# One-token attention with an MLP beside it, on one core: V taken in pairs, block sums masked on VectorE, activations stationary in the query and first MLP products

## The chip, the cores and the metric

The kernel runs on one core of a Trainium2 chip. The metric is the device time of one execution in microseconds (us). Three executions of the kernel before gave a median of 368.69 us (368.61 to 369.18). A profiled execution gives the trace; its own time is told beside its span below. Engines are named as the profile names them: PE (TensorE matmuls), PEld (its weight loads), DVE (VectorE), ACT (ScalarE), POOL (GpSimd), SP (SyncE), and a small q behind a name (SPq) for the engine's instruction queue.

## The reference, cut to what matters

Eight batch rows of one token, x of shape 8 x 576. Attention runs over the last W = 2048 positions of a cache with 16 key/value heads of 128 numbers; two query heads share a key/value head. Beside it runs an MLP with 4608 hidden units, and a gate g mixes the two.

```python
q = x @ wq                                   # 576 x 4096: 32 heads of 128
k, v = last 2048 positions of the caches     # 8 batches x 16 heads x 2048 x 128, bf16
p = softmax((q . k) * 128**-0.5)
a = (p . v) @ wo                             # 4096 x 576
h = gelu(layernorm(x) @ w1 + b1)             # 576 x 4608
b = h @ w2 + b2                              # 4608 x 576
g = sigmoid((x * gate_w).sum(-1))
out = g * a + (1 - g) * b
```

All tensors are bf16. The K and V stretches that are read make 134 MB, the weights some 20 MB; each byte is read once.

## The kernel before

**Units.** The 16 key/value heads are taken two at a time: 8 groups g, each of 4 quarters q. A quarter is one head with 4 batches and is one K transfer (line 648) and one V transfer (line 696) of 2048 KB each. All loads go from SP's queue into a ring of nine 2 MB slots (take_slot, lines 607 to 610); the transfer into a slot waits for what last read that slot (slot_free). The first slots of the ring are also where wq (lines 392, 393) and w1 (lines 395, 396) lie at the start, so the fourth to sixth K transfer wait for the query product and the transfers behind those for the first MLP product.

**K.** DVE transposes a K slot in two halves (L663) into a double buffer; for each half PE makes 8 matmuls of 128 x 512 (L680 loads weights, three follow on held weights from L173) that gather the scores of a group in four PSUM banks. The block-diagonal query blocks that stand in them are written by POOL, 4 copies a unit (L656). When a group is complete, DVE takes the maximum (L615) and joins it over the quarters, ACT makes the exponentials (L629), DVE transposes them into PT (L634) and the row sums go through PE (L638).

**V.** For one V slot PE makes 16 matmuls (L703), P's 32 columns stationary and 512 columns of V streaming, in turn in the four column strips of the array. Each strip gathers a quarter of the positions, and only some blocks of the result are wanted. ACT copies the bank out (L712, EV), and PE picks and adds the wanted blocks with eight-row selection matrices in f32 (L721, four calls a unit, selu). After four units ACT scales the group's output (L727), DVE transposes it (L730), and PE multiplies it with wo (AccGroup, L569, gathered in one PSUM bank over the whole kernel).

**The head and the MLP.** Lines 400 to 484 make the gate, the layernorm and the selection matrices. In the query product (L492, L494) and the first MLP product (L526, L528) a 128 x 128 block of weights is the stationary operand and 8 columns of the activation stream: 160 and 180 pairs of weight load and matmul. GELU runs on 128 x 288 (lines 533 to 548). w2 comes last, as four chunks of 9 row blocks; the last chunk is cut into transfers of 4, 3 and 2 blocks (line 760). Each block is two matmuls of 128 x 288 (L569) in two column strips. Then ACT and DVE copy the sum out (L782, L781) and two small transfers store it (L784).

**What sets the order.** The order of SP's transfers is a list (lines 576 to 588): K and V units in turn, with K five to six units ahead, a wo chunk after every eight V units, then b2 and w2. Every operation has a planned cost and a priority; schedule() (lines 62 to 144) puts each engine's operations in one fixed order by planned start, and emit() (lines 141 to 162) writes that order with semaphore waits. Nothing is reordered when it runs: an engine stands at the first operation whose wait isn't met.

```python
        while ki < NUQ or vi < NUQ:
            if ki < NUQ:
                stream.append(("K", ki))
                ki += 1
            if ki >= 6:
                stream.append(("V", vi))
```

Of the kernel before, what the change touches and what calls it, by code (L numbers as in the profile page):

```python
# [6 lines left out]
BF = mybir.dt.bfloat16  # L7
# [31 lines left out]
class _Plan:  # L39
# [101 lines left out]
    def emit(self, eng, handle, eng_sems, dma_sems, rec=None):  # L141
        known = {}
        for op in self.order[eng]:
            for d in op.deps:
                if d.is_dma:
                    sem, val, key = dma_sems[d.dma_sem], d.dma_val, ("dma", d.dma_sem)
                else:
                    sem, val, key = eng_sems[d.eng], d.milestone, ("eng", d.eng)
                    if d.eng == eng:
                        assert d.pos < op.pos, "same-engine dep must precede: %s -> %s" % (d.name, op.name)  # L150
                if known.get(key, 0) >= val:
                    continue
                handle.wait_ge(sem, val)
                known[key] = val
# [25 lines left out]
def build_kernel(nc, A_x, A_k_cache, A_v_cache, A_wq, A_wo, B_x, B_w1, B_b1, B_w2, B_b2, gate_w, out):  # L180
# [13 lines left out]
    FC, FJ = 4, 9  # L194
    FT = FC * FJ
    FCW = 128 * FJ
    WOR = 4
    NJ = 2
# [6 lines left out]
    with ExitStack() as es:  # L205
# [18 lines left out]
        req("ones_f", 128, F32)  # L224
# [4 lines left out]
        req("selu", 4 * 2 * 64, F32)  # L229
# [4 lines left out]
        req("sel", 4 * 128, BF)  # L234
        req("cols", 16, F32)
        req("xT", 6 * 8, BF)
        req("yT", 6 * 8, BF)
        req("qT", 256, BF)
        req("q4", 4 * 256, BF)
        req("qbd", 4 * 4 * 128, BF)  # L240
        req("b1T", FT, F32)
        req("b2", D, BF)
        req("u", FT * 8, F32)
        req("uh", FT * 8, F32)
        req("v1", FT * 8, F32)
        req("v2", FT * 8, F32)
        req("hT", FT * 8, BF)
        req("ob", 16, BF)
        req("ot32", 8, F32)
        req("gb", 16, F32)  # L250
# [5 lines left out]
        req("EV", 2 * 512, F32)  # L256
# [11 lines left out]
        over("b1c", "PT", 4480, FCW, BF)  # L268
# [22 lines left out]
        ones_f = view("ones_f")  # L291
# [6 lines left out]
        sel = view("sel").rearrange("p (h c) -> p h c", h=4)  # L298
        cols = view("cols")
        xT = view("xT").rearrange("p (t b) -> p t b", b=8)  # L300
        yT = view("yT").rearrange("p (t b) -> p t b", b=8)
        q4 = view("q4").rearrange("p (h m) -> p h m", h=4)
        qbd = view("qbd").rearrange("p (u h m) -> p u h m", u=4, h=4)
        b1T = view("b1T")
        b2_sb = view("b2", 8)
        u_sb, uh_sb, v1_sb, v2_sb = view("u"), view("uh"), view("v1"), view("v2")
        hT = view("hT").rearrange("p (t b) -> p t b", b=8)
        ob = view("ob", 8)
        ot32 = view("ot32", 8)
        gb = view("gb")  # L310
# [6 lines left out]
        selu = view("selu").rearrange("p (r u c) -> p r u c", r=4, u=2)  # L317
# [29 lines left out]
        BK_Q, BK_H, BK_X, BK_SEL = 4, 5, 6, 0  # L347
# [14 lines left out]
        o_onesf = add("pool", lambda e: e.memset(ones_f, 1.0), name="ones_f", cost=0.15)  # L362
# [13 lines left out]
        o_selb = []  # L376
        for he in range(4):
            def fn(e, he=he):
                src = bass.AP(arena, offset=aoffs("ident") + 64 * (he // 2) + he % 2, ap=[[AST, 128], [0, 4], [2, 32]])
                return e.tensor_copy(sel[:, he, :].rearrange("p (a i) -> p a i", a=4), src)  # L380
            o_selb.append(add("pool", fn, deps=[o_ident], name="selb%d" % he, cost=0.3))
        o_su0 = add("pool", lambda e: e.memset(view("selu"), 0.0), name="selu0", cost=0.5)
# [38 lines left out]
        o_dga = add("dve", lambda e: e.tensor_scalar(out=dg[:, 0:8], in0=idf8, scalar1=col(C_G, 8), scalar2=None, op0=ALU.mult), deps=[o_g, o_idf], name="dga", cost=0.12)  # L421
# [15 lines left out]
        def b1_fn(e):  # L437
            ins = None
            for j in range(FJ):
                src = bass.AP(arena, offset=aoffs("b1c") + j, ap=[[AST, FC], [FJ, 128]])  # L440
                ins = e.transpose(ps_bf[:, BK_X, 256 + 16 * j: 256 + 16 * j + FC], src, ident[0:FC, 0:FC])
            return ins
        o_b1p = add("pe", b1_fn, deps=db + [o_ident], name="b1_pe", cost=0.6, after=[o_xTp])

        def ev_T(dst, which):
            return lambda e: e.tensor_copy(dst, ps_bf[:, BK_X, which * 64: which * 64 + 48].rearrange("p (t b) -> p t b", b=8))
        o_xT = add("dve", ev_T(xT, 0), deps=[o_b1p], name="xT_ev", cost=0.2)

        def b1ev_fn(e):
            src = ps_bf[:, BK_X, 256:256 + 16 * FJ].rearrange("p (j c) -> p c j", j=FJ)[:, 0:FC, :]  # L450
            return e.tensor_copy(b1T.rearrange("p (c j) -> p c j", j=FJ), src)
        o_b1T = add("dve", b1ev_fn, deps=[o_b1p], name="b1T_ev", cost=0.15)
        o_yTp = add("pe", tr_in("y_bf", yz, 1), deps=[o_y, o_ident, o_xT, o_b1T] + o_yz, name="yT_pe", cost=0.6)
        def g_fn(e):
            e.matmul(ps[:, BK_X, 384:400], ones_f[0:8, :], dg[:, 0:16], start=True, stop=True)
            return e.matmul(ps[:, BK_X, 400:401], r8, col(C_G, 8), start=True, stop=True)
        o_gp = add("pe", g_fn, deps=[o_dga, o_dgb, o_onesf, o_g, o_r8], name="g_pe", cost=0.6, after=[o_yTp])
        o_yT = add("dve", ev_T(yT, 1), deps=[o_gp, o_yTp], name="yT_ev", cost=0.2)
        o_gb = add("dve", lambda e: e.tensor_copy(gb, ps[:, BK_X, 384:400]), deps=[o_gp], name="gb_ev", cost=0.15)
        o_gcol = add("dve", lambda e: e.tensor_copy(gcol, ps[:, BK_X, 400:401]), deps=[o_gp], name="gcol_ev", cost=0.15)  # L460
        o_obh = add("dve", lambda e: e.tensor_copy(ob[:, 0:8], dg[:, 8:16]), deps=[o_dgb], name="ob_hi", cost=0.12)
# [7 lines left out]
        o_selu, o_seln = [], []  # L469
        for u in range(2):  # L470
            for h in range(2):
                for r in range(4):
                    def fn(e, u=u, h=h, r=r):
                        dst = bass.AP(arena_f, offset=foffs("selu") + 128 * r + 64 * u + 32 * h + 4 * u, ap=[[AST // 2, 128], [8, 4], [1, 4]])
                        src = bass.AP(arena_f, offset=foffs("i32") + 8 * r + h, ap=[[AST // 2, 128], [0, 4], [2, 4]])
                        return e.tensor_copy(dst, src)
                    o_selu.append(add("pool", fn, deps=o_i32 + [o_su0], name="selu%d%d%d" % (u, h, r), cost=0.2, prio=-1))
        for l in range(2):
            for h in range(2):
                def fn(e, l=l, h=h):  # L480
                    dst = bass.AP(arena_f, offset=foffs("seln") + 64 * l + 32 * h, ap=[[AST // 2, 128], [8, 4], [1, 8]])
                    src = bass.AP(arena_f, offset=foffs("i32") + 16 * l + h, ap=[[AST // 2, 128], [0, 4], [2, 8]])
                    return e.tensor_copy(dst, src)
                o_seln.append(add("pool", fn, deps=o_i32, name="seln%d%d" % (l, h), cost=0.2, prio=-1))


        def q_fn(e):
            ins = None
            for hq in range(Hq):
                out_ = ps[:, BK_Q, hq * 8: hq * 8 + 8]  # L490
                for t in range(4):
                    ins = e.matmul(out_, wq_m[:, t, hq * 128:(hq + 1) * 128], xT[:, t, :], start=(t == 0), stop=False)  # L492
                c = hq % 16
                ins = e.matmul(out_, wq_r[:, c * 128:(c + 1) * 128], xT[:, 4 + hq // 16, :], start=False, stop=True)  # L494
            return ins
        o_qp = add("pe", q_fn, deps=dwq + [o_xT], name="q_pe", cost=9.0)

        def qT_fn(e):
            src = bass.AP(ps, offset=BK_Q * 512, ap=[[PST, 128], [16, 16], [1, 8], [8, 2]])
            return e.tensor_copy(view("qT").rearrange("p (l b h) -> p l b h", l=16, b=8), src)  # L500
        o_qT = add("dve", qT_fn, deps=[o_qp], name="qT_ev", cost=0.4)

        def sel_fn(e):
            ins = None
            for he in range(4):
                ins = e.matmul(ps[:, BK_SEL + he // 2, (he % 2) * 256:(he % 2) * 256 + 256], sel[:, he, :], view("qT"), start=True, stop=True)
            return ins
        o_selp = add("pe", sel_fn, deps=[o_qT] + o_selb, name="sel_pe", cost=0.6, prio=9)

        def q4_fn(e):  # L510
            return e.activation(out=view("q4"), in_=ps[:, BK_SEL:BK_SEL + 2, :].rearrange("p a n -> p (a n)"), func=ACTF.Copy)
        o_q4 = add("act", q4_fn, deps=[o_selp], name="q4_ev", cost=1.2)


        H_CH = 6
        o_hch = []
        for i0 in range(0, FT, H_CH):
            fts = list(range(i0, min(FT, i0 + H_CH)))
            def fn(e, fts=fts):
                ins = None  # L520
                for t in fts:
                    c, j = divmod(t, FJ)
                    out_ = ps[:, BK_H, t * 8: t * 8 + 8]
                    for kt in range(4):
# [330 lines left out]
```

## Time and profile before

| | |
|---|---|
| median of three executions | 368.69 us |
| profiled execution: its time | 369.14 us |
| profiled execution: its span | 367.4 us |
| mean granted PE clock | 0.875 |
| bytes moved by the DMA queues | 154.58 MB, mean 421 GB/s |
| weight loads recorded on PE | 1431 |
| matmuls recorded on PE | 1817 |

The span runs from the first to the last instruction; 1.74 us of the execution's time lie outside it. A busy time is the union of an engine's instructions. In the windows view a DMA share of 1.00 means that all 16 DMA engines move data, and the clock column is the share of full PE clock that was granted (1.00 or 0.50 at any moment). The chain view follows the work that ended last back from the end; in it, a row that begins with DMA lasts until the landing, and the row of the engine that waited for it stands next.

### The profile page before, as it was taken

The page shows a single profiled execution, that of the slowest core. Times are in us where ns is not written, and L with a number is a line of the kernel's source. Part 1 is how long each engine was busy: PE and PEld are TensorE (multiplying, and loading weights), DVE is VectorE, ACT ScalarE, POOL GpSimd, SP SyncE. Part 2 cuts the span into 40 slices and gives each one's busy share as a digit, 9 for nine tenths or more (in the row PEclk, how much of TensorE's full clock was granted, in tenths as well). Part 3 has the DMA queues.
Part 4 walks back from the last instruction along what each step waited for, and adds up shares of the span by engine and source line. Part 5 has one row for each costly group of instructions (what it writes and reads, how often), then busy time and mean ns, then how long its engine had stood idle before and what let it go on. Part 6 is the DMA issues. An engine that isn't in the chain of part 4 may idle for free.

```text
span 367.4 us, 4082 instructions
## 1 busy us (share of the span) xinstructions
PE 255.2 (69%) x1817; PEld 83.4 (23%) x1431; DVE 208.7 (57%) x253; ACT 48.0 (13%) x110; POOL 37.3 (10%) x170
## 2 busy tenths in 40 slices
PE   0359984798499398673996389656966399684776
PEld 0349200122032023010321023101211023113433
DVE  0704599698677754459654674478544775454000
ACT  1010000210310301003010301003100301003210
POOL 8141011011001000000000001100110000000000
PEclk9999999699699879887897869996996869976976
DMA  8999999999999999999999999999999999999994
GB/s 345 429 415 428 430 433 433 429 426 428 433 432 428 422 438 432 430 432 429 428 433 432 424 434 428 433 426 433 430 435 430 421 434 428 439 430 430 417 429 164
DMA packets 11850, 154.58 MB, mean 421 GB/s; under 512 B 1292, under 2 KB 1332, under 8 KB 3000
## 3 DMA queue, kind: packets, MB, share of 16 engines
q1 hardware_dynamic: 11776, 154.29, 98.5%
q8 instruction: 13, 0.21, 0.2%
q10 hardware_dynamic: 56, 0.03, 0.0%
q14 instruction: 5, 0.04, 0.0%
HBM read 154.31 MB, written 0.01 MB: 420 GB/s over the span
## 4 chain that ended last, share of the span: by engine, by line
DMA 67%; PE 17%; DVE 13%; issue 1%; ACT 1%; SPq 1%; DVEq 0%; ACTq 0%
DMA arena<-in_A_k_cache_dram 51%; DMA arena<-in_B_w_dram 15%; DVE arena L663 11%; PE ps L173 8%; PE ps L526 2%; PE ps L680 2%; PE ps L569 1%; DVE arena L615 1%; PE ps L721 1%; PE ps L703 1%; ACT arena L629 1%; PE ps L528 1%; DVE arena L624 0%; DVE arena L618 0%; SPq L395 0%
## 5 line engine op out<-in xcount | busy, mean ns | idle before, releaser
L663 DVE STREAM_TRANSPOSE arena<-arena 128x2048 f32<-128x2048 f32 x64 | 145.3, 2296 | 62.9 <-DMA arena<-in_A_k_cache_dram 57.2
L173 PE MATMUL ps<-arena 128*128 128x512 bf16 x402 | 135.5, 448 | 17.7 <-DVE arena L663 10.4
L680 PE MATMUL ps<-arena 128*128 128x512 bf16 x114 | 51.5, 452 | 13.3 <-DVE arena L663 13.3
L656 POOL COPY arena<-arena 32x32 bf16<-32x32 bf16 x128 | 26.2, 205 | 241.5 <-PE ps L173 231.2
L712 ACT ACTIVATE arena<-ps 128x512 f32<-128x512 f32 x32 | 19.2, 599 | 203.8 <-PE ps L703 203.8
L721 PE MATMUL ps<-arena 128*64 128x128 f32 x256 | 36.5, 291 | 9.6 <-ACT arena L712 7.7
L680 PEld LDWEIGHTS ps<-arena 128*128 128x128 bf16 x128 | 13.9, 109 | 120.5 <-issue 67.9
L703 PE MATMUL ps<-arena 128*32 128x512 bf16 x512 | 34.1, 382 | 3.3 <-DMA arena<-in_A_v_cache_dram 3.3
L721 PEld LDWEIGHTS ps<-arena 128*64 128x64 f32 x256 | 29.2, 144 | 25.4 <-ACT arena L712 14.0
L672 PE MATMUL ps<-arena 128*128 128x512 bf16 x6 | 3.5, 586 | 37.9 <-DVE arena L634 31.8
L615 DVE TENSOR_REDUCE arena<-ps 128x1 f32<-128x2048 f32 x8 | 18.3, 2282 | 20.3 <-PE ps L173 20.3
L629 ACT ACTIVATE arena<-ps,arena 128x512 bf16<-128x512 f32 x32 | 21.6, 686 | 41.0 <-DVE arena L624 41.0
L634 DVE STREAM_TRANSPOSE arena<-arena 128x512 bf16<-128x512 bf16 x32 | 19.9, 675 | 0.9 <-ACT arena L629 0.9
L703 PEld LDWEIGHTS ps<-arena 128*32 128x32 bf16 x512 | 11.4, 96 | 39.4 <-issue 26.4
L730 DVE STREAM_TRANSPOSE arena<-arena 128x128 bf16<-128x128 bf16 x8 | 2.6, 319 | 26.0 <-ACT arena L727 25.9
L569 PE MATMUL ps<-arena 128*8 128x288 bf16 (+1 forms) x140 | 14.1, 358 | 2.6 <-DMA arena<-in_B_w_dram 2.6
L526 PE MATMUL ps<-arena 128*128 128x8 bf16 x144 | 10.9, 201 | 4.2 <-DMA arena<-in_B_w_dram 4.2
L526 PEld LDWEIGHTS ps<-arena 128*128 128x128 bf16 x144 | 10.8, 159 | 4.7 <-DMA arena<-in_B_w_dram 4.7
L672 PEld LDWEIGHTS ps<-arena 128*128 128x128 bf16 x8 | 0.9, 107 | 46.1 <-DVE arena L634 39.5
L429 PE MATMUL ps<-arena 8*128 8x8 bf16 x8 | 0.5, 167 | 13.5 <-DVE arena L402 9.8
L569 PEld LDWEIGHTS ps<-arena 128*8 128x8 bf16 (+1 forms) x140 | 6.7, 102 | 12.5 <-issue 4.2
L640 DVE RECIPROCAL arena<-ps 128x1 f32<-128x1 f32 x8 | 1.4, 169 | 13.9 <-PE ps L638 13.9
(88 smaller groups left out, 93.5 us busy)
## 6 DMA issues: line engine op xcount, KB each, us to landing
arena<-in_A_k_cache_dram SPq DMA_DIRECT2D x32, 2048.0 KB, 34.5
arena<-in_A_v_cache_dram SPq DMA_DIRECT2D x32, 2048.0 KB, 35.5
arena<-in_B_w_dram SPq DMA_DIRECT2D x1, 4608.0 KB, 24.3
arena<-in_A_wo_dram SPq DMA_DIRECT2D x4, 1152.0 KB, 35.5
arena<-in_A_wq_dram SPq DMA_DIRECT2D x1, 4096.0 KB, 12.8
arena<-in_B_w_dram SPq DMA_DIRECT2D x3, 1296.0 KB, 33.6
arena<-in_B_w_dram SPq DMA_DIRECT2D x2, 576.0 KB, 28.4
arena<-in_A_wq_dram SPq DMA_DIRECT2D x1, 512.0 KB, 3.5
```

The source lines that it names most:

```text
L173: return e.add_instruction(mybir.InstMatmult(name=nc.get_next_instruction_name(), engine=mybir.EngineType.PE, ins=[e.lower_ap(rhs), e.lowe ...
L526: ins = e.matmul(out_, lhsT, yT[:, kt, :], start=(kt == 0), stop=False)
L569: ins = e.matmul(ps[32 * j:32 * j + 8, BK_ACC, 0:JN], lhsT, rhs[:, JN * j:JN * j + JN], start=False, stop=True, skip_group_check=True, til ...
L615: mx = add("dve", lambda e: e.tensor_reduce(out=k(MX), in_=ps[:, 0:4, :].rearrange("p a n -> p (a n)"), axis=AXL.X, op=ALU.max), deps=[qk_ ...
L629: return e.activation(out=Pm[:, 512 * c:512 * c + 512], in_=ps[:, c, :], func=ACTF.Exp, bias=k(NB), scale=SCALE, accum_out=k(SUM + c))
L634: pts.append(add("dve", (lambda c=c: lambda e: e.transpose(bass.AP(arena, offset=aoffs("PT") + 2048 * (g % 2) + 128 * c, ap=[[AST, 128], [ ...
L656: return e.tensor_copy(dst, src)
L663: tr = add("dve", (lambda h=h, kb=kb: lambda e: e.transpose(bass.AP(arena_f, offset=foffs("KT") + kb * 2048, ap=[[AST // 2, 128], [1, 2048]]),
L680: mm = e.matmul(*args, start=False, stop=last) if rc == 0 else held_matmul(nc, e, *args, stop=last)
L703: mm = e.matmul(ps[c:c + 32, BK_OS[i % 2], :], PT[:, g % 2, 512 * q + 32 * t:512 * q + 32 * t + 32], slot(s)[:, 512 * t:512 * t + 512], st ...
L712: u_ev[i] = add("act", lambda e: e.activation(out=EV[:, i % 2, :], in_=ps[:, BK_OS[i % 2], :], func=ACTF.Copy), deps=[prev] + ([u_sum[i - ...
L721: mm = e.matmul(osl, selu[:, r, q % 2, :], EV[:, i % 2, 128 * r:128 * r + 128], start=(q % 2 == 0 and r == 0), stop=(q % 2 == 1 and r == 3 ...
```

## The change

- **V in pairs.** The transfers come as six K, then two V, two K in turn. One V operation now does two units: 32 matmuls that alternate between two column strips, each strip with a unit of its own and all 16 position blocks in a row. All four units of a group land in one PSUM bank, and both slots of a pair come free when the pair is done.
- **Block sum on DVE.** ACT's copies (L712) and PE's f32 selections (L721) go. Once a group, four DVE operations on 128 x 128 multiply PSUM blocks with a column mask and add them; one f32 matmul a group (selv) then adds over partitions.
- **Activations stationary.** In the query and the first MLP products 32 columns of activations (8 used, the others zero) stand in a column strip and the weights stream, 512 or 384 columns at a time, four strips at once: 20 weight loads and 40 matmuls, and 20 and 60 (three more pairs bring in b1). The results come out with the batch on partitions: q goes through a DVE copy, a DVE transpose and four selections, GELU runs on 128 x 1152 (in part on ACT) and ends in a DVE transpose. The first K transpose now waits for the query's selection, whose data lie in its buffer.
- **w2** is cut into 12, 12 and 6 + 4 + 2 blocks, which fill three slots.
- **Waits.** emit() first gathers an operation's waits and keeps the largest one for each semaphore. POOL writes query blocks for two units at a time.

The core of the diff:

```diff
+            waits = {}
...
-                if known.get(key, 0) >= val:
-                    continue
+                if val > known.get(key, 0) and val > waits.get(key, (None, 0))[1]:
+                    waits[key] = (sem, val)
+            for key, (sem, val) in waits.items():
                 handle.wait_ge(sem, val)
                 known[key] = val
...
+        def held_x(e, out_of, lhs, rhs_of, n, t, first, last):
+            ins = None
+            for i in range(n):
+                for c in range(FC):
+                    if i == 0:
+                        ins = e.matmul(out_of(c, i), lhs(t, c), rhs_of(t, c, i), start=first, stop=last, skip_group_check=True, tile_position=(0, 32 * c))
+                    else:
+                        ins = held_matmul(nc, e, out_of(c, i), lhs(t, c), rhs_of(t, c, i), start=first, stop=last, skip=True, tile_size=(128, 32), tile_position=(0, 32 * c))
+            return ins
...
+                ins = held_x(e, lambda c, i: ps[32 * c:32 * c + 32, BK_Q + i, :], lambda t, c: xT[:, t if t < 4 else 4 + c // 2, :], rhs_of, 2, t, t == 0, t == 4)
...
+                ins = held_x(e, lambda c, i: ps[32 * c:32 * c + 32, BK_H + i, 0:HW_], lambda t, c: yT[:, t if t < 4 else 4 + c // 2, :], rhs_of, HN, t, False, t == 4)
...
-        stream = [("K", i) for i in range(5)]
...
+        stream = [("K", i) for i in range(6)]
+        for vi in range(0, NUQ, 2):
+            stream += [("V", vi), ("V", vi + 1)]
+            if (vi + 2) % (NUQ // (Hq // WO_CH)) == 0:
+                stream.append(("W", vi // (NUQ // (Hq // WO_CH))))
+            stream += [("K", i) for i in (vi + 6, vi + 7) if i < NUQ]
+        M_CUTS = [[12], [12], [6, 4, 2]]
+        stream += [("B", 0)] + [("M", i) for i in range(len(M_CUTS))]
...
-                deps = [d] + ([qk_half[n - 2]] if n >= 2 else [o_y, o_ssq])
+                deps = [d] + ([qk_half[n - 2]] if n >= 2 else [o_selp])
...
+            if i % 2 == 0:
+                return
...
                 for t in range(16):
-                    c = 32 * (t % 4)
-                    mm = e.matmul(ps[c:c + 32, BK_OS[i % 2], :], PT[:, g % 2, 512 * q + 32 * t:512 * q + 32 * t + 32], slot(s)[:, 512 * t:512 * t + 512],
-                                  start=(t < 4), stop=(t >= 12), skip_group_check=True, tile_position=(0, c))
+                    for j in (i - 1, i):
+                        c = 32 * (j % 4)
+                        mm = e.matmul(ps[c:c + 32, BK_OS[g % 2], :], PT[:, g % 2, 16 * c + 32 * t:16 * c + 32 * t + 32], slot(v_load[j][0])[:, 512 * t:512 * t + 512],
+                                      start=(t == 0), stop=(t == 15), skip_group_check=True, tile_position=(0, c))
...
-            u_ev[i] = add("act", lambda e: e.activation(out=EV[:, i % 2, :], in_=ps[:, BK_OS[i % 2], :], func=ACTF.Copy),
...
                 for r in range(4):
-                    mm = e.matmul(osl, selu[:, r, q % 2, :], EV[:, i % 2, 128 * r:128 * r + 128],
...
+                        src = ps[:, BK_OS[g % 2], 128 * r:128 * r + 128]
+                        if r == 0:
+                            return e.tensor_scalar(out=EV[:, g % 2, :], in0=src, scalar1=maskr[:, 0:1], scalar2=None, op0=ALU.mult)
+                        return e.scalar_tensor_tensor(out=EV[:, g % 2, :], in0=src, scalar=maskr[:, r:r + 1], in1=EV[:, g % 2, :], op0=ALU.mult, op1=ALU.add)
...
+                u_sum[g] = add("pe", lambda e: e.matmul(ps[:, BK_S, OC + 128 * (g % 2):OC + 128 * (g % 2) + 128], selv, EV[:, g % 2, :], start=True, stop=True),
```

288 lines of the change are left out of this document (122 added, 166 removed).

## The prediction, made before the changed kernel ran

> **What bounds the kernel now.** First the profile's page: spans and busy times, the DMA row of the 40 slices, the queues, the time from issue to landing.
>
> ```profile
> span 367.4 us, 4082 instructions
> PE 255.2 (69%) x1817; PEld 83.4 (23%) x1431; DVE 208.7 (57%) x253; ACT 48.0 (13%) x110; POOL 37.3 (10%) x170
> ...
> DMA  8999999999999999999999999999999999999994
> ...
> q1 hardware_dynamic: 11776, 154.29, 98.5%
> q8 instruction: 13, 0.21, 0.2%
> ...
> arena<-in_A_v_cache_dram SPq DMA_DIRECT2D x32, 2048.0 KB, 35.5
> ```
>
> No engine is busy over 69%; the loads fill the 16 DMA engines for 98.5% of the span. A transfer is issued 35.5 us before it lands, seven units of K or V ahead. What the engines do is hidden unless it makes a slot late by more than that lead, or comes after the last load. So I look for time in two places only: how long the stream of loads is, and what follows its end.
>
> The chain of waits shows when some transfers had landed on all engines, since the DVE transpose or the PE product that waited starts then.
>
> ```profile
> 137.46 2.32 DVE arena L663
> ...
> 186.24 4.51 DVE arena L663 x2
> ...
> 227.90 4.52 DVE arena L663 x2
> ...
> 277.91 4.52 DVE arena L663 x2
> ...
> 319.48 2.32 DVE arena L663
> ...
> 360.85 4.17 PE ps L569 x36
> ```
>
> By the order of the stream, 137.46 to 186.24 and 227.90 to 277.91 hold ten units each: 48.78 and 50.01 us, 1.23 us apart for the same bytes. 186.24 to 227.90 and 277.91 to 319.48 hold eight units and a wo chunk each: 41.66 and 41.57, the same. One event made the second stretch late. The DMA view cut to windows (0 to 227.9, then 227.9 to 250) shows what shares the engines with the loads:
>
> ```profile
> q8 instruction: 8, 0.13, 0.2%
> ```
> ```profile
> q8 instruction: 1, 0.02, 0.2%
> ```
>
> These are packets of 16 KB on one queue. PE's instructions are most of the program, and 3248 recorded ones over 13 packets are one per 250, so I take q8 for PE's program being fetched. 0.2% of 16 engines over 22.1 us is 0.7 us (0.5 to 0.9 with the rounding): a packet occupies one engine for about that, and that engine's share of every later load comes later. The first eight packets left the landings at an even pace; the ninth cost 1.23 us. My reading: the fetches go round eight engines, each of the first eight makes another engine late by about the same, and the ninth is the first to hit an engine already late. That needs no more than what the rows show, but the rows don't name engines.
>
> The end, in windows of 1 us, in order of time, and in the view of the w2 transfers (L763):
>
> ```profile
> 360.00:361.00 1.00, 0.22 (x4) 0.09 (x4) 0.00 (x0) 0.00 (x0) 0.00 (x0) 0.50 0.85 342
> 361.00:362.00 1.00, 1.00 (x10) 0.53 (x8) 0.00 (x0) 0.00 (x0) 0.00 (x0) 0.50 0.56 227
> 362.00:363.00 1.00, 1.00 (x12) 0.57 (x10) 0.00 (x0) 0.00 (x0) 0.00 (x0) 0.50 0.35 142
> 363.00:364.00 1.00, 1.00 (x12) 0.57 (x10) 0.00 (x0) 0.00 (x0) 0.00 (x0) 0.50 0.14 55
> 364.00:365.00 1.00, 1.00 (x12) 0.41 (x8) 0.00 (x0) 0.00 (x0) 0.00 (x0) 0.74 0.00 0
> ```
> ```profile
> 348.79 1.05 PE L703 MATMUL ps<-arena 128*32 128x512 bf16 x16 [1.76 <-DMA arena<-in_A_v_cache_dram]
> ...
> 360.85 4.15 PE L569 MATMUL ps<-arena 128*8 128x288 bf16 x36 [0.78 <-DMA arena<-in_B_w_dram]
> 365.12 0.40 ACT L782 ACTIVATE arena<-ps 8x288 bf16<-8x288 f32 x1 [12.49 <-PE ps L569]
> ```
> ```profile
> L763 SPq DMA_DIRECT2D arena<-in_B_w_dram x6: 328/2713/4215, 317.2 to 337.2; - x6
> ...
> DMA to landing us min/median/max: 26.8/31.8/37.4
> ```
>
> The engines end one after another, from 0.85 busy at 360 to none at 364: a spread of over 3 us, as if the worst had two packets more than the best. The last piece, issued at 337.2, lands 26.8 later: 364.0. PE's last 18 blocks run without a gap from 360.85 to 365.0 at half clock, 0.23 us a block of two matmuls. So the end is: last landing at 364.0, 1.0 of PE backlog, 2.4 to the span's end at 367.4, and 1.74 outside the span: 369.14. The median of the runs is 0.45 lower, and I carry that over.
>
> **The change part by part.** *The loads.* The bytes are the same. A K slot is freed as before. The first V slot of a pair is held 4.88 us more (48.78 / 10) until its twin lands, and both until 32 matmuls are through. Matmul pace, from pairs of rows at full and at half clock, with the granted clock around the last V unit below them:
>
> ```profile
> 305.31 0.40 PE L680 MATMUL ps<-arena 128*128 128x512 bf16 x1
> ...
> 306.22 0.39 PE L680 MATMUL ps<-arena 128*128 128x512 bf16 x1
> ```
> ```profile
> 323.53 0.63 PE L680 MATMUL ps<-arena 128*128 128x512 bf16 x1
> ...
> 325.24 0.63 PE L680 MATMUL ps<-arena 128*128 128x512 bf16 x1
> ```
> ```profile
> 347.46:350.87 3.41, 1.38 (x19) 0.67 (x20) 0.00 (x0) 0.60 (x1) 0.00 (x0) 1.00 1.03 433
> 350.87:354.28 3.41, 3.41 (x25) 1.85 (x25) 0.31 (x1) 0.37 (x1) 0.00 (x0) 0.50 1.03 440
> ```
>
> Four in 0.91 us are 0.23 each, four in 1.71 are 0.43. Sixteen in 1.05 (348.79) are four deep, so the four strips ran side by side. In a pair each of two strips is 16 deep: 3.6 to 6.9 us for two units, where 2.1 was spent. A V slot is freed 7 to 11 us later than now, out of a lead of 35.5: no starvation, cost 0 while that lead is there. If it were gone, each late slot would cost what it is late by.
>
> *Engines in mid-stream.* Terms per unit, group, or call:
>
> ```profile
> L721 PE MATMUL ps<-arena 128*64 128x128 f32 x256 | 36.5, 291 | 9.6 <-ACT arena L712 7.7 <-DVE arena L640 1.9
> ...
> L712 ACT ACTIVATE arena<-ps 128x512 f32<-128x512 f32 x32 | 19.2, 599 | 203.8 <-PE ps L703 203.8
> ...
> L727 ACT ACTIVATE arena<-ps,arena 128x128 bf16<-128x128 f32 x8 | 2.9, 368 | 22.7 <-PE ps L721 22.7
> L730 DVE STREAM_TRANSPOSE arena<-arena 128x128 bf16<-128x128 bf16 x8 | 2.6, 319 | 26.0 <-ACT arena L727 25.9
> ...
> L535 DVE TENSOR_TENSOR arena<-ps,arena 128x288 f32<-128x288 f32 x1 | 0.5, 458 | 1.7 <-PE ps L528 1.7
> ```
>
> PE loses L721's 36.5 (16 of 256 pairs stay) and gains 16 x (3.6 - 2.1) = 24 at full clock, 77 at half: even then a group's 68 K products at 0.43 and two pairs at 6.9 make 43 us against 41.6 of loads, and where PE was busiest it had the full clock:
>
> ```profile
> 30.00:60.00 30.00, 27.15 (x211) 10.30 (x161) 23.19 (x16) 0.89 (x2) 2.92 (x15) 1.00 1.01 431
> ```
>
> ACT loses 19.2. DVE gains 32 sums; none such is in the trace, so I bound one by L535's 0.46 and that cut to the width (128 of 288: 0.20), and take 0.3, near L730 with its 0.32: 10 us on 209. All of it lies beside the loads: cost 0. Fewer waits and POOL's writes by twos: 0, for the same reason.
>
> *Head.* q and h take 40 and 63 matmuls for 160 and 180, and give the first slots back earlier; the new DVE steps (a copy, a transpose, GELU four times as wide) come while six K units are under way. The DMA row is at 9 from the second slice on: neither gain nor loss, 0. If that cover were gone, the new DVE work would count: GELU's four steps alone, at L535's 0.46 and four times the width, are 7 us.
>
> *PE's program.* Weight loads and matmuls by the code: 1431 + 1839 before, 882 + 1350 after (V's 512 pairs stay, L721 loses 240 pairs, q and h lose 297 loads and 237 matmuls net, the rest is b1 and small). 2232 is 0.68 of 3270: "a third less" is so. At one packet per 250 that is 8.9 packets, some waits on top: the ninth stands on the edge. When the ninth packet came, this had run:
>
> ```profile
> 0.00:240.50 240.50, 168.24 (x1224) 53.49 (x944) 149.72 (x178) 29.45 (x67) 33.21 (x150) 0.90 1.00 426
> ```
>
> 2168 of PE's instructions, which after is 50 to 64 before its last (some of 1839 matmuls have no record). The last twelve w2 blocks are 48 instructions, so the ninth would come near the end of the second chunk's products, at 359 to 360. It would find an engine with some 2 us of loads left, and make it late as now. Then the last landing is about where it is: 363.8 to 364.0. Without it: 364.0 - 1.23 = 362.8.
>
> [...]
>
> *The end.* Twelve blocks lie in the three last pieces, nine before. A block is 147 KB, 0.34 us at the 430 GB/s or so of the rows above. The second chunk lands at 362.8 - 4.1 = 358.7 if its engine was not yet hit. At half clock PE is through it at 361.4, through the six at 362.8, waits for the four until 363.2, ends them at 364.1 and the two at 364.6. At full clock it ends at 364.3, just behind the landing. So 364.3 to 364.6 for 365.0. I take 364.4.
>
> Sum: 369.14 - 0.6 = 368.5 for a profiled execution, **368.1** for the median.
>
> **The rivals.**
> *B, no second hit.* The waits are few enough, or the packet comes too late. Last landing 362.8; PE at half clock ends at 358.7 + 24 x 0.23 = 364.2, at full clock at 363.1. Time 366.8 to 367.9. For it: 8.9 is under nine, against it: by my count of the code's dependencies some 80 waits beyond the first of an operation stand on PE's queue, and they are instructions of its program too.
> *C, slower: the last group comes late.* PE's fixed order has the last group's wo product ahead of the w2 chunks. After the last V unit lands (347.5 to 348.8) come 3.6 to 6.9 of matmuls, 4 x 0.3 on DVE, an f32 selection of 0.6 to 1.0, 0.37 (L727), 0.32 (L730), about 0.6 of semaphores and 0.9 for the product: done at 355 to 360. The first chunk lands at 354.6. From there 36 blocks take 8.3 at half clock: if PE stands at half clock and starts them after 356.5, it decides the end, at up to 368: 369.5 to 371.5. With 4.3 at full clock it doesn't. The rows at 347.46 and 350.87 show half clock behind a stretch that was 40% busy, and the pairs leave PE idle just there. [...]
> *D, the lateness isn't from fetches.* Then the last landing stays at 364.0, the chunk of twelve lands at 359.9, and at half clock PE ends at 365.4: 369.1, or 368.0 at full clock.
>
> **How the numbers follow.** Forecast 0.48 (367.8 to 368.6), B 0.26 (around 367.3), C 0.14 (around 370), D 0.12. About 0.2% (0.74 us) is what a measurement of this kernel can tell from no change: faster means under 367.95. That is B and about a third of the forecast: 0.42. Slower means over 369.43: C, 0.14. The rest, 0.44, is within. The range leaves out the lowest tenth (B at full clock) and the upper part of C: 366.9 to 369.8.
>
> **What would show it.** q8 with nine packets, the ninth after 355 (eight: B). DMA share 1.00 until about 360. Landings of K units ten apart 48.8 us apart everywhere, with no 50.0. PE's last product ending within 0.6 of the last landing. Wrong would be: a DMA share below 0.95 in any slice between the second and the last (a late slot), or PE without a gap from the last V unit on (C).

## The result and the profile after

The changed kernel took 367.41 us (median of 7 runs, 367.14 to 367.98), the kernel before 368.67 on the same chip (7 runs, 368.50 to 369.29): a ratio of 0.9965, 95% interval 0.9955 to 0.9974. That is 1.26 us or 0.35% faster, inside the predicted range, near its lower end, and 0.7 below the predicted 368.1. The profiled execution took 367.57, with a span of 365.5 (369.14 and 367.4 before): the span is 1.9 shorter, and 2.07 instead of 1.74 lie outside it.

The page of the kernel after, in the order of the rows that were shown of before:

```profile
span 365.5 us, 2939 instructions
...
PE 246.3 (67%) x1350; PEld 57.8 (16%) x882; DVE 225.7 (62%) x285; ACT 31.9 (9%) x82; POOL 36.1 (10%) x156
...
DMA  8999999999999999999999999999999999999995
...
q1 hardware_dynamic: 11632, 154.29, 99.0%
q8 instruction: 9, 0.15, 0.1%
...
arena<-in_A_k_cache_dram SPq DMA_DIRECT2D x32, 2048.0 KB, 35.0
arena<-in_A_v_cache_dram SPq DMA_DIRECT2D x32, 2048.0 KB, 33.4
```

PE has nearly a third fewer instructions but only 9 us less to do, DVE 17 more, ACT 16 less, and none of that is seen in the DMA row: from the second slice to the last but one it stands at 9, as before. The loads' queue (q1) moves the same 154.29 MB. What is new is q8, nine packets for thirteen, and when they come. The DMA view cut to 0 to 361, then to 361 to 365:

```profile
q8 instruction: 8, 0.13, 0.1%
```
```profile
q8 instruction: 1, 0.02, 1.5%
```

Eight come before 361; the ninth comes when only the last piece of w2 is still on its way. The chain of waits of the kernel after gives start, length and cause; a DMA row ends at the landing on all engines:

```profile
90.42 34.59 DMA arena<-in_A_v_cache_dram
...
129.39 37.28 DMA arena<-in_A_v_cache_dram
...
171.85 34.03 DMA arena<-in_A_v_cache_dram
...
211.94 35.51 DMA arena<-in_A_v_cache_dram
...
252.94 33.41 DMA arena<-in_A_v_cache_dram
...
290.72 37.31 DMA arena<-in_A_v_cache_dram
...
333.05 29.68 DMA arena<-in_B_w_dram
...
363.23 0.45 DVE arena L759
```

The V landings are at 125.01, 166.67, 205.88, 247.45, 286.35 and 328.03. Two groups apart they stand 80.87, 80.78, 80.47 and 80.58 us from each other: even within 0.4, with no step of 1.23 in any stretch. The row at 333.05 is the last piece of w2: landed at 362.73, 1.2 before the 364.0 of before. The last 1-us windows (PE, its weight loads, DVE, ACT, POOL, the granted clock, the DMA share, GB/s) and the timeline of the tail:

```profile
360.00:361.00 1.00, 0.55 (x10) 0.26 (x8) 0.00 (x0) 0.00 (x0) 0.00 (x0) 1.00 0.96 392
361.00:362.00 1.00, 0.58 (x10) 0.20 (x6) 0.00 (x0) 0.00 (x0) 0.00 (x0) 1.00 0.57 226
362.00:363.00 1.00, 0.88 (x12) 0.37 (x12) 0.00 (x0) 0.00 (x0) 0.00 (x0) 1.00 0.12 37
363.00:364.00 1.00, 0.18 (x4) 0.00 (x0) 0.45 (x1) 0.40 (x1) 0.00 (x0) 1.00 0.00 0
```
```profile
355.58 2.13 PE L550 MATMUL ps<-arena 128*8 128x288 bf16 x32 [0.47 <-DVE arena L707]
...
358.59 1.64 PE L550 MATMUL ps<-arena 128*8 128x288 bf16 x24 [0.88 <-DMA arena<-in_B_w_dram]
...
360.68 0.90 PE L550 MATMUL ps<-arena 128*8 128x288 bf16 x12 [0.45 <-DMA arena<-in_B_w_dram]
...
362.07 1.11 PE L550 MATMUL ps<-arena 128*8 128x288 bf16 x12 [0.49 <-DMA arena<-in_B_w_dram]
363.23 0.40 ACT L760 ACTIVATE arena<-ps 8x288 bf16<-8x288 f32 x1 [8.05 <-PE ps L550]
```

The DMA engines still begin to fall idle at 360 to 361 (0.96, before 0.85), but the share is down to 0.12 in the window from 362, where before had 0.35 and a further 0.14 after 363. PE has the full clock and waits for each piece; its last product ends at 363.18, 0.45 behind the last landing. Before it ended at 365.0. From there to the span's end it is 2.3, and 2.4 before.

So the gain lies at one place, the end: the slowest DMA engine is done 1.2 us earlier, and PE has less left over behind it.

### The profile page after: what moved, and what is told of

Read it like the earlier page. It is cut to its first block, busy times and chain, and to the rows that moved or that the text cites. A ratio compares the mean times of both kernels' runs of the same rounds, so it can differ in the third digit from the quotient of the medians.

```text
span 365.5 us, 2939 instructions
## 1 busy us (share of the span) xinstructions
PE 246.3 (67%) x1350; PEld 57.8 (16%) x882; DVE 225.7 (62%) x285; ACT 31.9 (9%) x82; POOL 36.1 (10%) x156
## 3 DMA queue, kind: packets, MB, share of 16 engines
q1 hardware_dynamic: 11632, 154.29, 99.0%
## 4 chain that ended last, share of the span: by engine, by line
DMA 73%; PE 14%; DVE 10%; issue 1%; SPq 1%; ACT 0%; DVEq 0%
DMA arena<-in_A_v_cache_dram 58%; DMA arena<-in_B_w_dram 15%; PE ps L684 9%; DVE arena L641 7%; PE ps L175 3%; PE ps L658 1%; DVE arena L592 1%; DVE arena L533 1%; PE ps L472 0%; SPq L673 0%; DVE arena L528 0%; DVE arena L532 0%; DVE arena L530 0%; PE ps L550 0%; ACT arena L526 0%
## 5 line engine op out<-in xcount | busy, mean ns | idle before, releaser
L175 PE MATMUL ps<-arena 128*128 128x512 bf16 (+2 forms) x468 | 135.1, 441 | 0.0
L684 PE MATMUL ps<-arena 128*32 128x512 bf16 x512 | 67.1, 422 | 21.4 <-DMA arena<-in_A_v_cache_dram 21.4
L658 PE MATMUL ps<-arena 128*128 128x512 bf16 x128 | 54.2, 424 | 24.3 <-DVE arena L641 24.3
L684 PEld LDWEIGHTS ps<-arena 128*32 128x32 bf16 x512 | 28.7, 105 | 68.1 <-issue 48.7
L658 PEld LDWEIGHTS ps<-arena 128*128 128x128 bf16 x128 | 13.5, 105 | 140.5 <-DVE arena L641 71.3
L650 PE MATMUL ps<-arena 128*128 128x512 bf16 x8 | 4.6, 575 | 24.3 <-DVE arena L611 14.0
L615 PE MATMUL ps<-arena 128*128 128x1 f32 x16 | 4.0, 317 | 18.4 <-DVE arena L614 18.4
L698 DVE SCALAR_TENSOR_TENSOR arena<-ps,arena 128x128 f32<-128x128 f32 x24 | 8.4, 351 | 0.9
L615 PEld LDWEIGHTS ps<-arena 128*128 128x128 f32 x16 | 3.9, 287 | 24.7 <-DVE arena L614 21.4
L704 ACT ACTIVATE arena<-ps,arena 128x128 bf16<-128x128 f32 x8 | 2.9, 367 | 54.3 <-PE ps L700 54.3
L700 PE MATMUL ps<-arena 128*128 128x128 f32 x16 | 5.1, 414 | 3.4 <-DVE arena L617 1.8
```

Source lines behind the costliest of these rows:

```text
L175: return e.add_instruction(mybir.InstMatmult(name=nc.get_next_instruction_name(), engine=mybir.EngineType.PE, ins=[e.lower_ap(rhs), e.lowe ...
L615: sp_ = add("pe", lambda e: e.matmul(ps[:, BK_S, 0:1], seln, k(S), start=True, stop=True), deps=[s_] + o_seln + b6_r[-2:], after=b6_w[-1:] ...
L658: mm = e.matmul(*args, start=False, stop=last) if rc == 0 else held_matmul(nc, e, *args, stop=last)
L684: mm = e.matmul(ps[c:c + 32, BK_OS[g % 2], :], PT[:, g % 2, 16 * c + 32 * t:16 * c + 32 * t + 32], slot(v_load[j][0])[:, 512 * t:512 * t + ...
L698: return e.scalar_tensor_tensor(out=EV[:, g % 2, :], in0=src, scalar=maskr[:, r:r + 1], in1=EV[:, g % 2, :], op0=ALU.mult, op1=ALU.add)
L700: u_sum[g] = add("pe", lambda e: e.matmul(ps[:, BK_S, OC + 128 * (g % 2):OC + 128 * (g % 2) + 128], selv, EV[:, g % 2, :], start=True, sto ...
```

## The experiments

**Theory**: each packet of PE's program makes one DMA engine late by about a microsecond (the 1.23 us of before), eight packets reach eight different engines, and the ninth, if it comes while loads are left, is the first to come to a late one; the seventeenth would be the third on one engine. **Rivals**: the new order of the transfers makes the end earlier; or PE's shorter backlog at the end (its clock, the cut of w2) does; or the lateness has nothing to do with fetches. "First to last" below is the time between the first and the last engine's landing of the last transfer, read from the landing events of the trace: 3.13 us before, 1.91 after. Ratios are to the kernel before on the same chip (368.68 to 368.97).

**e1, the program padded back.** 37 pairs of a zero weight load and a one-column matmul ahead of every V pair but the last two: 518 pairs.

```diff
+                for _ in range(37 if i < 28 else 0):
+                    e.matmul(ps[0:32, BK_ACC, 400:401], zeros_bf[:, 0:32], zeros_bf[:, 0:1], start=True, stop=True, skip_group_check=True, tile_position=(0, 0))
```

> The changed kernel with 1036 more PE instructions (518 pairs of a weight load and a one-column product of zeros into unused PSUM columns, 37 pairs ahead of the matmuls of each V pair but the last two); transfers and results stay. Fetch theory (a second instruction packet on one DMA engine sets the last landing): q8 has 12 or 13 packets as in the kernel before, the last w2 piece lands at 363.9 to 364.3 in place of 362.7, the time is 368.4 to 368.9 against 367.4, about that of the kernel before. Rival, the gain is from the order of the transfers: landing 362.7, time 367.4. Rival, the gain is all PE's end: landing 362.7, time 367.4 to 367.6. If 518 pairs at 0.1 us cost PE its cover, slices of the DMA share fall under 0.95 and the time passes 369.5.

Measured 368.55 (ratio 0.9996, 0.9987 to 1.0005): the whole gain is gone. The page, the DMA view of 266 to 267, and the end:

```profile
q8 instruction: 13, 0.21, 0.2%
```
```profile
q8 instruction: 1, 0.02, 5.5%
```
```profile
336.31 27.45 DMA arena<-in_B_w_dram
...
364.26 0.45 DVE arena L761
```

Thirteen packets, the ninth at 266; the last piece landed at 363.76, 1.0 later than in the kernel after, and first to last is 2.98. The pads cost PE 10 us of busy time in mid-stream (256.7 for 246.3), but that can't be the cause: no slice of the DMA row between the first and the last fell below 9, as in the kernel after.

**e2, a tenth of the pads, all early.** 50 pairs ahead of the first V pair only, near 72 us, some 290 us before the last landing.

```diff
+                for _ in range(50 if i == 1 else 0):
```

> The changed kernel with only 100 more PE instructions (50 such pairs ahead of the first V pair's matmuls, some 5 us of PE near 70 us, where PE is a third idle). Fetch theory: still nine packets, but the ninth comes 100 instructions earlier, near 350 to 356 in place of 362.1, finds an engine with loads left, and the last landing moves from 362.7 to 363.8 to 364.1: time 368.3 to 368.7, over 1 us slower for work that lies 290 us ahead of the end. Both rivals (order of transfers, PE's end): 367.4 within 0.2.

Measured 368.57 (0.9996, 0.9988 to 1.0005): a hundred instructions that were long over cost as much as a thousand. The DMA view of 360 to 361, the windows and the timeline:

```profile
q8 instruction: 1, 0.02, 6.0%
```
```profile
360.00:361.00 1.00, 1.00 (x22) 0.72 (x18) 0.00 (x0) 0.00 (x0) 0.00 (x0) 1.00 0.88 348
361.00:362.00 1.00, 1.00 (x22) 0.74 (x18) 0.00 (x0) 0.00 (x0) 0.00 (x0) 1.00 0.52 194
362.00:363.00 1.00, 0.38 (x8) 0.06 (x2) 0.00 (x0) 0.00 (x0) 0.00 (x0) 1.00 0.08 32
363.00:364.00 1.00, 0.79 (x12) 0.37 (x12) 0.00 (x0) 0.00 (x0) 0.00 (x0) 1.00 0.03 12
```
```profile
363.18 1.10 PE L550 MATMUL ps<-arena 128*8 128x288 bf16 x12 [0.80 <-DMA arena<-in_B_w_dram]
364.33 0.40 ACT L762 ACTIVATE arena<-ps 8x288 bf16<-8x288 f32 x1 [8.14 <-PE ps L550]
```

The packet came at 360.10 and took until 361.06: the last landing up to then, at 360.46, was 1.93 from first to last, the next 3.22. Then a share of 0.08 and of 0.03 for over a microsecond: 0.06 is one engine of 16. The landing events say the same: of the last transfer's 16, fifteen come within 1.91 and one at 3.19. A single late engine has the last landing, PE waits 0.80 for the four-block piece with the full clock, and the end moves by 1.1. The packet had been expected at 350 to 356; it came when PE had 2286 recorded instructions behind it, against 2252 at the ninth packet of the kernel after. Why later was not tried.

**e5, a second dose.** 80 pairs ahead of the same V pairs as in e1: 1120 pairs.

```diff
+                for _ in range(80 if i < 28 else 0):
```

> The changed kernel with 2240 more PE instructions (1120 pairs of a weight load and a one-column product of zeros, 80 ahead of each V pair but the last two). Fetch theory, now as a dose: 17 packets, the seventeenth is the third on one engine, so the last landing moves by another 1.2 us, to 365.0 to 365.3, and the time to 369.6 to 370.0 (one hit 367.4, two 368.6). Rival, a program beyond some length costs its 1.2 once: 368.5. If PE loses its cover (some 20 us more of PE work), DMA slices fall under 0.95.

Measured 370.10 (1.0033, 1.0020 to 1.0046), 0.1 above the theory's range, with the last landing inside it. The DMA view of 0 to 352.4 and of 352 to 353, then the timeline:

```profile
q8 instruction: 16, 0.26, 0.3%
```
```profile
q8 instruction: 1, 0.02, 6.0%
```
```profile
364.48 1.12 PE L550 MATMUL ps<-arena 128*8 128x288 bf16 x12 [0.47 <-DMA arena<-in_B_w_dram]
365.64 0.40 ACT L762 ACTIVATE arena<-ps 8x288 bf16<-8x288 f32 x1 [7.96 <-PE ps L550]
```

Seventeen packets, the last at 352.52; the last landing at 365.15 and first to last 4.39. So the ends by packets that came in time are: eight 362.73 (after), nine (e2) 363.83, thirteen (e1, the last of them at 361.96) 363.76, seventeen 365.15; the last two figures of first to last, 2.98 and 4.39, are steps from 1.91. It goes by rounds of eight, not by packets.

The trace has more on the rounds. Of the 16 landings of e5's last transfer, seven come within 0.71 of the first, one at 2.06, seven at 2.85 to 3.15 and one at 4.39: which reads as seventeen packets, two on each of seven engines and three on an eighth. In the kernel before seven come within 0.75, one at 1.44, three at 1.55 to 1.78 and five at 2.88 to 3.13: which reads as thirteen packets, one on each of three engines and two on each of five. What made the single ones at 2.06 and 1.44 late stays open. And the time that a packet takes repeats after eight: in e5 0.96, 0.96, 0.95, 0.88, 0.88, 0.94, 0.94 and 0.93 us, then the same eight within 0.01, then 0.96.

**e4, the kernel before with a shorter PE program.** It leaves out four fifths of the query and first MLP products, three quarters of the block selections, and 12 of the 16 V matmuls of the first 16 units; all transfers and their order stay.

```diff
-                for t in range(16):
+                for t in range(4 if i < 16 else 16):
...
-                for r in range(4):
+                for r in range(1):
```

> The kernel before, all transfers and their order as they are, with PE work left out: one of five products in the query and the first MLP matmuls, one of four in the block selection, and 4 of 16 V matmuls in the first half; some 1960 weight loads and matmuls are left of 3270. Fetch theory: seven or eight packets, no engine hit twice, the last landing at 362.7 in place of 364.0, the time 367.3 to 368.0 with PE's end as in the kernel before (0.5 to 1.1 after the landing). Rival, the order of the transfers or the pairs matter: landing 364.0. Rival, PE's end: landing 364.0, time 368.2 to 368.7.

Measured 367.71 (0.9974, 0.9966 to 0.9983). Its page has `q8 instruction: 8, 0.13, 0.1%`, the last of them at 360.27. The windows of the end:

```profile
361.00:362.00 1.00, 1.00 (x12) 0.55 (x10) 0.00 (x0) 0.00 (x0) 0.00 (x0) 0.50 0.55 203
362.00:363.00 1.00, 1.00 (x14) 0.59 (x12) 0.00 (x0) 0.00 (x0) 0.00 (x0) 0.67 0.04 14
```

With the order of before the last landing is at 362.94: the share is down to 0.04 where before had 0.35. So the order of the transfers isn't what makes the end earlier. PE, at half clock (0.50) up to 362 and then partly at full clock (0.67 in the mean), ends at 363.6, 0.4 later than in the kernel after, 0.2 of it with the landing: no more than that is its tail worth here.

**e3, the old cut of w2** in the kernel after.

```diff
-        M_CUTS = [[12], [12], [6, 4, 2]]
+        M_CUTS = [[9], [9], [9], [4, 3, 2]]
```

> The changed kernel with w2 cut as before (9, 9, 9 and 4 + 3 + 2 blocks). Fetch theory: the last landing stays at 362.7; PE's last product ends 0.4 to 0.6 after it at full clock and up to 1.1 at half, so 367.4 to 368.0. Rival, the gain is all from the cut of w2: 368.4 to 368.7.

Measured 367.66 (0.9965, 0.9948 to 0.9981): 0.25 above the kernel after in the medians, and the same ratio to before. Last landing 362.89, PE's end 363.34. The gain isn't from the cut; what smaller share it has, the interval of 0.6 either way can't tell.

**e6 and e7, one half of the change each.** e6 is the kernel before with V in pairs and the block sum on DVE; e7 is the kernel after with V taken back to single units, ACT's copies and PE's selections.

```diff
-        stream = [("K", i) for i in range(5)]
+        stream = [("K", i) for i in range(6)]
+        for vi in range(0, NUQ, 2):
+            stream += [("V", vi), ("V", vi + 1)]
...
+            v_load[i] = (s, d)
+            if i % 2 == 0:
+                return
```

(e6 against before; e7 has the same lines the other way round against after.)

> The kernel before with the V part of the change alone (order of the transfers, V pairs, block sum on DVE, POOL's writes by twos); query and first MLP products, w2 cut and waits as before. Some 2900 PE instructions are left of 3360. Fetch theory: 11 packets, second hits stay, the last landing at 363.8 to 364.1, the time within 0.3 of the kernel before (368.4 to 369.0). Rival, the gain belongs to the V part: 367.4. Additive shares of the gain by instructions removed: 368.1.

> The changed kernel with the V part taken back (transfers in turn, one V unit at a time, ACT's copies and PE's f32 selections); stationary activations, w2 cut and gathered waits stay. Some 2720 PE instructions. Fetch theory: 10 packets, last landing 363.8 to 364.1, time 368.2 to 368.7. Rival, the gain belongs to this part: 367.4. Additive shares: 368.0.

Measured: e6 368.60 (0.9992, 0.9983 to 1.0001) with eleven packets, e7 368.56 (0.9995, 0.9985 to 1.0005) with ten. Neither half gains anything that can be told from nothing; both together gain 1.26. The timelines, e7 and then e6:

```profile
363.59 1.10 PE L554 MATMUL ps<-arena 128*8 128x288 bf16 x12 [0.47 <-DMA arena<-in_B_w_dram]
```
```profile
357.43 7.11 PE L565 MATMUL ps<-arena 8*8 8x288 bf16 x84
```

e7 is plain: PE waits for the piece that landed at 363.54; the last landing is at 364.23, 0.1 past what was expected. e6 isn't: the last landing is late too (364.08), but PE has no gap from 357.43 to 364.5, after the last V pair had come to an end mostly at half clock (0.58 in the mean of 353 to 355) and left it idle for 1.6. That is the start of the prediction's rival C, and in e6 it ends together with the late landing. How much e6 would have had without one of the two was not tried.

**e8, the old waits** in the kernel after: emit() writes every wait again, 112 wait instructions on PE in place of 44 and 38 in place of 3 on SP, as the traces record them.

```diff
-                if val > known.get(key, 0) and val > waits.get(key, (None, 0))[1]:
-                    waits[key] = (sem, val)
-            for key, (sem, val) in waits.items():
+                if known.get(key, 0) >= val:
+                    continue
                 handle.wait_ge(sem, val)
```

> The changed kernel with emit() as before alone: 112 wait instructions on PE for 44, 38 on SP for 3, all else the same. Fetch theory: PE's program is 68 instructions longer, so the ninth packet comes in the second w2 chunk's products, at 359 to 360.5 in place of 362.1, and the last landing moves to 363.8 to 364.0: time 368.3 to 368.7. Rival, a wait costs its own time on the path that ends last: four or five of them at the end, under 0.1 each, 367.4 to 367.7, landing 362.7.

Measured 368.45 (0.9992, 0.9984 to 1.0001): without the gathered waits the gain is gone, but not in the way expected. PE's ninth packet came at 361.42 and added 0.5 to first to last. Most of the lateness had come 28 us earlier, with a packet of another queue of instructions, q14, in the DMA view of 320 to 340; the timeline of the end stands below it:

```profile
q8 instruction: 1, 0.02, 0.3%
q14 instruction: 1, 0.01, 0.1%
```
```profile
357.76 6.87 PE L548 MATMUL ps<-arena 128*8 128x288 bf16 x80 [0.47 <-DVE arena L705]
```

The q14 packet (8 KB) at 333.26 fell between two landings whose first to last went from 2.1 to 3.1: it came to an engine that was already late. The kernel after has a q14 packet at 336.08 that left first to last as it was (1.95 and 1.97). Which engine's program q14 carries, the rows don't say. PE, too, has hardly a gap from 357.76 on. So e8 has a late landing (364.18) and a late PE, and they can't be parted here.

**e9, a try for a better version.** The last two-block piece of w2 by 16 transfers of 8 partitions, to give the engines that are free early the last work.

```diff
+                    for p in range(0, 128, 8):
+                        d = dma("sp", (lambda j=j, jn=jn, at=at, p=p: lambda e: e.dma_start(slot(s)[p:p + 8, at * D:(at + jn) * D], src[p:p + 8, j * D:(j + jn) * D]))(),
+                                "t2", 8 * jn * D * 2, name="d_w2_%d_%d_%d" % (ci, n, p), after=last_dma[-1:])
```

> The kernel after, with the last two-block piece of w2 loaded by 16 transfers of 8 partitions each in place of one of 128 partitions. Fetch theory: eight of the 16 DMA engines are behind by one program packet each at the end (first to last landing 1.9 us apart in the kernel after), the other eight are free at 360.8. Whether a transfer of 8 partitions spreads over all 16 engines, no row here shows. If the small ones go to eight engines only, and those are the ones that are free early, the last landing comes some 0.6 earlier (362.1 for 362.73) and the time is about 366.9; if they are the late ones, it comes some 0.7 later (363.4) and the time is about 368.0; if they spread over all 16, nothing moves: 367.4. A rival by which the engines' lateness is an even spread that belongs to the loads themselves gives a later landing whenever eight engines alone carry the piece, and never an earlier one.

Measured 370.78 (1.0053, 1.0040 to 1.0067), beyond all three cases. Its windows:

```profile
362.00:363.00 1.00, 0.06 (x4) 0.05 (x4) 0.00 (x0) 0.00 (x0) 0.00 (x0) 1.00 0.28 76
363.00:364.00 1.00, 0.61 (x8) 0.23 (x8) 0.00 (x0) 0.00 (x0) 0.00 (x0) 1.00 0.07 18
```

The engines are mostly idle and nothing is finished: the last transfers land one after another, 0.4 to 1.3 us apart, until 365.88. The price goes with the many small transfers; the ninth q8 packet came earlier too, at 361.28, and its part in it was not parted off. What the test was for, which engines are late, stays open. A kernel that beats the changed one was not found.

## Why the prediction was right and where it was wrong

**The sign and the range held, and it was rival B that came about.** The likeliest case was 368.1 with a second hit at 359 to 360. B had been given 0.26 and the forecast 0.48, so the range held by a rival that it included, not by the likeliest case. B, at full PE clock, had PE's end at 363.1 and the landing at 362.8; measured were 363.18 and 362.73. Of B's 366.8 the measured 367.41 differs by what lies outside the span (0.33 more) and by the gap of the profiled run to the median (0.16 where 0.45 was carried over). One sign was too weak: nine packets with the ninth after 355 were to mark the forecast and eight to mark B; nine came, the ninth after 355, and it was B.

**The step that failed** is in "PE's program": "the ninth would come near the end of the second chunk's products, at 359 to 360". The time was not the fault, the instruction was. The kernel after, up to 359.60 and up to the packet:

```profile
0.00:359.60 359.60, 243.68 (x1320) 56.75 (x854) 225.26 (x284) 31.46 (x81) 36.14 (x156) 0.86 1.00 427
0.00:362.06 362.06, 245.20 (x1338) 57.45 (x870) 225.26 (x284) 31.46 (x81) 36.14 (x156) 0.86 1.00 427
```

The count of 2168 weight loads and matmuls was indeed reached at 359.6, but the packet came after 2208 of them. With the wait instructions that the trace has on PE, before had run 2235 instructions at its ninth packet and after 2252: nearly the same. e8 shows that waits count: its ninth came after 2146 weight loads and matmuls, 62 fewer than in the kernel after, and 112 waits, 2258 together. The waits are the term that was mis-sized. Taking over the count of 2168 from before took over its 67 waits too, and the argument against B counted on some 80; the kernel after has 44 in all. That is 23 of the 40 instructions. The other 17 were beyond what the count could place: some matmuls of before have no record, and over the ten kernels with a ninth packet it came after 2223 to 2323 recorded instructions. And 40 instructions are 2.5 us, since PE stands at the last pieces' landings. At 362.06 hardly a load was left to be late; in e2 a packet 2 us sooner cost 1.1, so the gain hangs on a narrow margin.

**The fetch reading stood.** Rival D falls: e2 moved the last landing by 1.1 with 50 pairs of a weight load and a zero matmul 290 us earlier, and e5 moved it by a further 1.3 to 1.4. The 1.23 us of the chain of before came back as the 1.2 by which the last landing is earlier. The rounds of eight are shown by the doses, by the counts of late landings and by the packets' times; no row names an engine, so that each round takes the same eight in the same order is argued from these. Landings missed their expected ranges by 0.1 to 0.2 in e1, e3, e4, e7 and e8, the time by 0.1 in e5; e9 alone was far off.

The size of a fetch shows in the rows: packets of 16 KB, nine for the 2278 instructions recorded on PE and thirteen for 3339 before, 253 and 257 a packet. Whether PE loses time to a fetch, no row here says; the stream of loads, which fills the DMA engines (q1 for 99.0% of the span), lost 1.1 us by one in e2.

**The covers held.** No slice of the DMA row fell, so the pairs' longer slots, the query and MLP steps at the head and DVE's sums cost nothing, as costed. The sizes, from the groups and the tail's timeline of the kernel after:

```profile
L697 DVE TENSOR_SCALAR arena<-ps,arena 128x128 f32<-128x128 f32 x8 | 2.7, 340 | 26.8 <-PE ps L684 26.8
...
L698 DVE SCALAR_TENSOR_TENSOR arena<-ps,arena 128x128 f32<-128x128 f32 x24 | 8.4, 351 | 0.9
```
```profile
347.62 4.41 PE L684 MATMUL ps<-arena 128*32 128x512 bf16 x26 [3.23 <-DMA arena<-in_A_v_cache_dram]
```

DVE's sums take 0.34 and 0.35 each where 0.3 was taken: 11.1 us for 10. The last V pair was done at 352.7, some 5 us after its start and well inside the 3.6 to 6.9.

**Rival C** did not come about, but nearer than its 0.14: the wo product began at 355.58, 1.15 after the first w2 chunk had landed and before the 356.5 from which C would decide at half clock. PE had the full clock by then (1.00 in every 2-us window from 351 to 359). From the pair's end to the wo product it took 2.9 us, where the prediction's terms add to 3.1 to 3.5; its 0.6 of semaphores rests on no row that it shows, and in the timeline of the kernel after the steps themselves take 2.64, which leaves 0.26 for all handovers between the engines. In e6 and e8 PE began its last stretch without a gap at 357.4 and 357.8, with a mean clock of 0.50 to 0.78 up to 361, and was part of the end.

**The end.** The forecast's PE end of 364.3 to 364.6 is what e2, with its second hit, shows: 364.3. The new cut of w2, which the prediction costed together with the rest, is worth nothing that e3 can tell from its spread.

## What to carry to other kernels

Where the DMA engines are full from start to end, look at what else uses them. Here it was the program's own instructions (q8: thirteen packets of 16 KB before, nine after, each 0.9 to 1.0 us on one engine), and the slowest engine, not their mean, set the end: in e2 one landing of 16 came 1.28 behind the other fifteen and moved the end by 1.1. What mattered then was how many fetches came before the last load, in rounds of eight, so that each half of the shortening gained nothing that can be told from nothing (e6, e7) and both together 1.26 us; instructions that do nothing, such as waits that another wait includes, counted too (e8: with 68 more of them the ninth packet came 62 weight loads and matmuls sooner). Whether another kernel's fetches come in such rounds, its own trace has to show. To place one, count every instruction of the queue, waits with them, allow for a spread (100 instructions here), and ask where the engine will stand when it gets there.

## What the runs showed of the hardware

- A packet of q8 or q14 takes one engine for 0.9 or 0.3 us (0.88 to 0.97 and 0.31 within the spans of before and after), but the landings that follow are 1.0 to 1.3 us later on it where it can be seen alone (e2: first to last 1.93 to 3.22; e8: 2.1 to 3.1 for a packet half as large). That lateness is hardly made up for: in before first to last was 3.08 behind the ninth packet and 2.95 some 30 us later, ahead of the tenth, and in the kernel after it stands at 1.9 to 2.0 from 213 us to the end.
- Time outside the span differs between kernels. In the medians over the executions of each it is 1.73 to 1.76 in before, e4, e6, e7 and e8, and 1.91 to 2.06 in the kernel after, e1, e2, e3, e5 and e9. The gathered waits alone don't explain it, since e7 has them. In the traces each of the six has a q14 packet after the span's end (at 367.31 in the kernel after); before, e4, e6 and e8 have none, and e7's profiled execution, with 1.99 outside, has a q8 packet there (368.17). Whether such a fetch is the cause was not tried. A span that is 1.9 shorter is therefore no time that is 1.9 shorter.
- Sixteen small transfers behind one another on SP's queue went with an end 3 us later for the same 288 KB (e9: last landing at 365.88 for 362.73).
